# Attention and a greedy mixture of experts on one core: route 1's logits ahead of a branch, another form of the threshold rounds, another order of the first weight steps, and two GpSimd drains

## The chip, the core and the metric

The kernel runs on one core of a Trainium2 chip. Its engines are TensorE (PE, matrix products; its weight loads are listed as PEld), VectorE (DVE), ScalarE (ACT), GpSimd (POOL) and SyncE (SP), which issues most DMAs; each works through its own queue in order. The metric is the device time of one execution in microseconds, as the median of several runs.

## The reference

Eight batches of eight heads, 576 positions of 64 elements, go through attention with a mask in blocks of 64. The result, as 4608 tokens of 512, goes through a mixture of eight experts with a greedy assignment: all 4608 × 8 logits are walked through in falling order, and a token goes to an expert if it has none yet and the expert has fewer than 576 tokens.

```python
# attention: scores = q k^T / 8, masked where block(i) < block(j); softmax; times v
x = attn_out.transpose(0, 2, 1, 3).reshape(4608, 512)
logits = x @ w_gate
for idx in np.argsort(-logits.flatten()):
    tok, e = idx // 8, idx % 8
    if assigned[tok] >= 0 or counts[e] >= 576: continue
    assigned[tok] = e; counts[e] += 1
for e in range(8):
    mask = assigned == e
    out[mask] = np.maximum(x[mask] @ w1[e], 0.0) @ w2[e]   # 512 -> 1024 -> 512
```

## The kernel before, in words

**Attention** takes about the first 342 us. It leaves x in DRAM as two 16-bit halves (high and low) and the logits in SBUF as 128 partitions × 36 tokens × 8 experts. No line of it is changed.

**Eight routes** then give each expert its tokens, one expert a route. Every token proposes itself to the best expert that is still open. Route k finds for each open expert the 576th largest proposed logit, takes the expert whose threshold is highest, marks its tokens, and takes them and the expert out of the logits (`Lm`) for route k+1. The threshold is found in `rounds`: 14 rounds, each cuts an interval to a quarter. One round is: three thresholds (`cd`, L782 on DVE); how many logits lie above each, counted per partition by two DVE instructions (`jk`, L790, with the counts by accumulation) and one ACT instruction (`ja`, L759); the sums over partitions on PE (`tot`, L806); the choice of the step from them (`sg`, L809, DVE). `CB` (L792) is the lower end of the interval, which grows by the step chosen. In round 6 the search goes over to a shifted copy of the logits (`m_P`). Route 0 has another form: four quick rounds and a test whether they suffice, then a branch (`If`, L942) whose rarely taken side has the other rounds. Route 7 needs no rounds.

**From marks to rows**: `place` and `invert` turn the marks into a list of 576 token numbers by PE products (`pe` L977, `ps` L984) and DVE steps (`OH`, `OL`, `RH`, `ixt`, `ix`; RH is the last operand of `pe` on DVE). POOL gathers the rows in five indirect DMAs of 128 (the last of 64) rows (`xg`, L1050). For experts 0 and 1 PE transposes them (`xt`, L1062) and DVE (L1067) and ACT (L1066) copy them out as `X`; for the others SP's DMA transposes.

**Weights** of an expert come in 12 pieces of 512 KB from SP's DMAs (`raw`, L990) and are split into 16-bit halves. The first four pieces of experts 0 and 1 are split by one ACT step each (L1007) and one DVE step (L1009); all others by ACT (L1014, L1018) and POOL (L1020). For expert 0 the first four pieces are asked for as soon as its number is known, ahead of the branch.

**FFN** of an expert: `h` on PE (L1102, three passes over halves) in two groups of columns (128 and 448 for expert 0, else 256 and 320), its relu as halves `HH` by ACT (L1088) and `HL` by DVE (L1090), then `y` on PE (L1127, and L1131 for the 64 rows of tile m=4), out of PSUM by ACT (L1110) and for m=4 also DVE (L1114), and a scatter to the output on POOL, an indirect DMA per tile m (L1118). The last expert takes its tiles in the order 0, 1, 2, 4, 3.

**Order.** The kernel writes each engine's order itself: every piece of work is a generator whose `yield` names an engine, a cost in ns and events to wait for, and a greedy list scheduler `Sched` picks what is issued next by costs, events and priorities (a smaller number goes first). Costs, event times (`sc.ev`) and `sc.busy` change nothing but the order. Route k+1 and expert k+1's weights are worked on beside the FFN of expert k, so their instructions stand among each other in the queues; waiting is done by semaphores.

**Before the change at the branch**: route 0's index list is made (the `invert` ahead of L942), the result of the test is loaded (`values_load`, L970), and all engines concerned branch. Behind it come eight warming matmuls (L953), the weight steps of expert 0, the gathers and X copies; a generator `out` (made in `route`) waits until the fourth weight piece of expert 0 is split, then takes the chosen expert and its tokens out of `Lm` (L913 to L930) and starts route 1, which begins with the best open logit per token (`vm`, L728), proposals (`nP` L744, `PV` L746), and their transposed copy `PB`, by PE (`rt`, L750), ACT (L754) and DVE (L751).

## Time and profile before

| | |
|---|---|
| timed runs | 788.42, 785.0, 785.38 us; median 785.38 |
| profiled execution, its own time | 788.48 us |
| its span, first to last instruction | 786.6 us |
| mean granted PE clock in it | 0.969 |
| attention | about 0 to 342 us |
| first h of the experts 0, 1, 2, 3 | 365.27, 427.25, 480.95, 531.46 us |
| index product `pe` of routes 0 and 1 | 357.53, 411.78 us |
| last scatter issued; last instruction | 778.18; 786.6 us |

A row of the timeline reads: start, duration, engine, line, operation, output <- input, shapes, count, and in brackets the idle time ahead of it with what ended it. Neighbouring equal instructions are shown as one row. In a row of stretches stand start and end, length, then busy time with instruction count for PE, PEld, DVE, ACT and POOL, the granted PE clock, the share of DMA engines in use, and GB/s. Some rows show a name with "q" behind the engine: instructions of its sequencer, such as a wait, a drain or a branch. Line numbers in brackets of the form L1118 belong to the kernel before; the changed kernel's are up to 16 higher or one lower.

### The profile page before, as it was taken

How to read it: one execution, taken by the hardware profiler on the slowest of the kernel's cores; microseconds unless marked ns; L12 is line 12 of the kernel's file. 1: busy time of each engine (PE TensorE's matmuls, PEld its weight loads, DVE VectorE, ACT ScalarE, POOL GpSimd, SP SyncE). 2: the span in 40 equal slices, each digit the busy share in tenths (PEclk: the TensorE clock that was granted, in tenths of full speed). 3: DMA queues.
4: the chain of work that ended last, by engine and by line, in shares of the span. 5: the costliest groups of instructions: out<-in, count | busy, mean ns of one | idle time of the engine just before them, and what ended most of it. 6: DMA issues, size and time to landing. Idle time of an engine off the chain costs nothing.

```text
span 786.6 us, 19035 instructions
## 1 busy us (share of the span) xinstructions
PE 724.0 (92%) x6532; PEld 480.4 (61%) x6532; DVE 563.5 (72%) x2295; ACT 540.7 (69%) x1456; POOL 465.2 (59%) x515
## 2 busy tenths in 40 slices
PE   5789998899989999957997999999999999999995
PEld 3566776667766777735544756647557475574752
DVE  6899788998899879666988878969688692430210
ACT  5788878888988898735835859495965948391210
POOL 5788887898889877512414348184661927675001
PEclk9899999999999999977997999999999999999998
DMA  9879999989999994258026066391935719771001
GB/s 202 162 151 176 213 193 209 157 158 226 195 213 168 224 187 90 77 124 273 9 95 237 5 235 154 125 246 47 291 92 186 177 68 279 237 172 50 22 22 38
DMA packets 244354, 121.66 MB, mean 155 GB/s; under 512 B 200832, under 2 KB 227328, under 8 KB 244256
## 3 DMA queue, kind: packets, MB, share of 16 engines
q1 hardware_dynamic: 238320, 101.42, 57.0%
q0 software_dynamic: 5936, 19.01, 7.5%
q8 instruction: 52, 0.85, 0.5%
q14 instruction: 46, 0.38, 0.1%
HBM read 71.45 MB, written 18.87 MB: 115 GB/s over the span
## 4 chain that ended last, share of the span: by engine, by line
PE 40%; DMA 6%; POOL 3%; ACT 2%; issue 2%; DVE 1%; SPq 0%; POOLq 0%; ACTq 0%
PE h L1102 22%; PE y L1127 14%; DMA raw<-in_moe_w_dram 4%; PE y L1131 3%; POOL W L1020 1%; POOL xg L1050 1%; DMA xg<-x,ix 1%; ACT W L1018 1%; PE pe L977 1%; ACT ja L759 1%; ACT raw L1014 1%; PE tot L806 0%; DMA out_dram<-yo,ix 0%; SPq L990 0%; ACT HH L1088 0%
## 5 line engine op out<-in xcount | busy, mean ns | idle before, releaser
L438 POOL TENSOR_TENSOR P<-P,m 128x320 f32<-128x320 f32 (+8 forms) x285 | 208.6, 766 | 51.4 <-DVE m L430 34.6
L1102 PE MATMUL h<-X,W 128*128 128x320 f16 (+3 forms) x1536 | 198.5, 289 | 0.2 <-DVE HL L1090 0.2
L1102 PEld LDWEIGHTS <-W 128*128 128x128 f16 x1536 | 142.7, 98 | 42.8 <-issue 1.5
L416 ACT ACTIVATE P<-psb,m 128x576 f32<-128x576 f32 (+8 forms) x288 | 149.2, 542 | 26.3 <-DVE m L409 17.3
L1127 PE MATMUL y<-W,HH 128*128 128x512 f16 x512 | 152.4, 379 | 0.0
L1020 POOL TENSOR_TENSOR W<-raw,W 128x1024 f16<-128x1024 f32 x56 | 118.2, 2135 | 30.0 <-ACT W L1018 26.2
L405 DVE TENSOR_REDUCE m<-psb 128x1 f32<-128x576 f32 (+8 forms) x288 | 125.1, 481 | 14.5 <-PE psb L380 14.0
L463 PE MATMUL psb<-mident,P 128*128 128x128 f32 x800 | 107.0, 283 | 11.0 <-POOL P L438 3.8
L380 PEld LDWEIGHTS <-qT 128*64 128x64 f16 x1408 | 78.8, 114 | 44.1 <-issue 29.3
L1118 POOL DMA_INDIRECT out_dram<-yo,ix x40 | 38.8, 970 | 108.6 <-ACT yo L1110 71.9
L380 PE MATMUL psb<-kT,qT 128*64 128x288 f16 (+8 forms) x704 | 92.9, 289 | 9.8 <-ACT P L416 9.3
L463 PEld LDWEIGHTS psb<-mident,P 128*128 128x128 f32 x800 | 88.1, 143 | 22.6 <-POOL P L438 6.6
L498 PE MATMUL psb<-PT,V 128*64 128x448 f32 (+5 forms) x776 | 98.1, 391 | 2.2 <-DVE PT L446 1.7
L1088 ACT ACTIVATE HH<-h 128x320 f16<-128x320 f32 (+3 forms) x128 | 51.8, 408 | 67.1 <-PE h L1102 59.8
L1127 PE MATMUL y<-W,HL 128*128 128x512 f16 x256 | 97.1, 379 | 0.0
L1050 POOL DMA_INDIRECT xg<-x,ix x40 | 39.9, 999 | 90.6 <-DMA raw<-in_moe_w_dram 48.1
L444 ACT ACTIVATE PT<-psb 128x512 f32<-128x512 f32 (+1 forms) x165 | 82.7, 592 | 6.6 <-PE psb L463 6.2
L380 PE MATMUL psb<-kS,qT 128*64 128x288 f16 (+8 forms) x704 | 85.4, 287 | 1.7 <-DVE kS L350 1.5
L1090 DVE SCALAR_TENSOR_TENSOR HL<-h,HH 128x320 f16<-128x320 f32 (+3 forms) x128 | 57.5, 452 | 39.3 <-ACT HH L1088 39.1
L1127 PEld LDWEIGHTS <-HH 128*128 128x128 f16 x512 | 46.8, 97 | 52.6 <-issue 1.7
L1014 ACT ACTIVATE raw<-raw 128x512 f32<-128x512 f32 x112 | 67.4, 624 | 8.1 <-DMA raw<-in_moe_w_dram 8.1
L498 PEld LDWEIGHTS psb<-PT,V 128*64 128x64 f32 x776 | 49.8, 138 | 33.3 <-issue 24.3
(234 smaller groups left out, 1038.9 us busy)
## 6 DMA issues: line engine op xcount, KB each, us to landing
raw<-in_moe_w_dram SPq DMA_DIRECT2D x64, 512.0 KB, 5.5
x<-XR SPq DMA_DIRECT2D x8, 1152.0 KB, 5.5
kn<-in_k_dram SPq DMA_DIRECT2D x15, 576.0 KB, 4.9
qn<-in_q_dram SPq DMA_DIRECT2D x15, 576.0 KB, 7.2
V<-in_v_dram SPq DMA_DIRECT2D x64, 128.0 KB, 4.4
V<-in_v_dram SPq DMA_DIRECT2D x16, 64.0 KB, 3.7
xg<-x,ix POOLq DMA_INDIRECT x41, 4.4
out_dram<-yo,ix POOLq DMA_INDIRECT x40, 2.8
```

Source lines behind the costliest of these rows:

```text
L380: nc.tensor.matmul(out if len(K1.shape) == 2 else out.rearrange("p (r j) -> p r j", r=2), lhsT=A[:, h, 64 * i:64 * i + 64], rhs=K1, start= ...
L405: nc.vector.tensor_reduce(m[:, 0, c:c + 1], ps[:, o:o + 64 * (i + 1)] if g else s.part(ps, g, i, o), axis=AX.X if g else AX.XY, op=OP.max)
L416: nc.scalar.activation(out, in_, AF.Exp, bias=m[:, 1, c:c + 1], scale=s.ESC, accum_out=m[:, 2, c:c + 1])
L438: nc.gpsimd.tensor_tensor(sl, sl, m[:, 3, c:c + 1].to_broadcast([P, w]), op=OP.mult)
L444: s.nc.scalar.activation(out, in_, AF.Copy)
L463: nc.tensor.transpose(ps[:, a], s.Pb[n % s.NP][:, s.OFF[i] + 128 * j:s.OFF[i] + 128 * j + P], s.ident)
L498: nc.tensor.matmul(ps[64 * h:64 * h + 64, 64 * (i0 - b0):64 * (b1 - b0)], lhsT=vn[:, j, 2 * (n % 2) + h, :], rhs=pt[:, s.PTI[(j, i0)]:s.PT ...
L1014: nc.scalar.activation(raw[:,x],raw[:,x],AF.Copy,scale=s.WS)
L1020: nc.gpsimd.tensor_tensor(lw,raw,hi,op=OP.subtract)
L1090: nc.vector.scalar_tensor_tensor(HL[:,f,ts],ps,0.0,HH[:,f,ts],op0=OP.max,op1=OP.subtract)
L1102: nc.tensor.matmul(ps,lhsT=W[:,a,d,f*P:f*P+P],rhs=X[:,4*(d//2)+d%2+l,ts],start=(d==0 and n==0),stop=(d==3 and n==2))
L1127: if m<4: nc.tensor.matmul(ps,lhsT=Z[:,f,m*P:m*P+P],rhs=Y[:,a,f],start=(f==n==0),stop=(f==7 and n==2))
```

## The change

1. **Rounds** of routes 1 to 6: each threshold used to be lower end + step + multiple of the width, in three instructions after the step `sg` is known. Now the three sums without the step (`base`, `bs`) are made at the end of the round before, by three instructions from that round's thresholds (three memsets in round 6, where the search starts from zero again), and after `sg` one instruction adds the step to all three. It has an accumulator output that is not used. The lower end `CB` is no longer kept from round to round, but made from the first threshold in rounds 6 and 13.
2. **Route 1's logits**: `winner` makes them (in a tile of their own, `L_1`) and the best per token ahead of the branch, on DVE between RH and the copy of `pe`; the branch's other side makes them again after its own rounds. Behind the branch route 1 starts at once. Two waits given to the scheduler for route 1, and 1500 ns in PE's account, are gone.
3. **First weights' steps**: other times, costs and priorities in the scheduler, which put the ACT and DVE splits of expert 0's first four pieces elsewhere among the X copies.
4. **Drains**: after the m=4 scatter of the last two experts POOL executes a `drain`.

```diff
--- before.py
+++ after.py
@@ route @@
-        yield D,369 if k else 30,('Lm',k),('mid',k-2),('wc',0,s.GW) if k==1 and s.GW>=0 else None
-        if k: V.tensor_reduce(vm,Lm,axis=AX.X,op=OP.max)
+        yield D,369 if k>1 else 30,('Lm',k),('mid',k-2)
+        if k>1: V.tensor_reduce(vm,Lm,axis=AX.X,op=OP.max)
...
-                yield T,214,'rt',('xm',0,s.GS) if k==1 and s.GS>=0 else None
+                yield T,214,'rt'
@@ rounds @@
-                        yield D,70 if k==0 else 210,('P2',k) if PBx is not PB else None
+                        yield D,70 if k==0 else 140,('P2',k) if PBx is not PB else None
                         if k==0: V.tensor_tensor(cand[:,2:3],base[:,2:3],nw,op=OP.add)
-                        else:
-                            for i in (2,0,1): V.tensor_scalar(cand[:,i:i+1],lo,nw,(i+1)*w,op0=OP.add,op1=OP.add)
+                        else: V.tensor_scalar(cand,base,nw,0.0,op0=OP.add,op1=OP.add,accum_out=s.ab)
...
-                    if t: add(lo,lo,nw)
+                    if k:
+                        if t==s.NSC: V.tensor_scalar(CB[:,0:1],cand[:,0:1],-w,None,op0=OP.add)
+                        if t==s.NS-1: V.tensor_scalar(CB[:,1:2],cand[:,0:1],-w,None,op0=OP.add)
+                    elif t: add(lo,lo,nw)
...
                     if t==s.NS-1: add(CB[:,2:3],CB[:,0:1],lo)
-                    elif k==0:
+                    else:
                         base=rp.tile([P,3],F32,tag="base",name=f"bs{k}_{t}")
-                        V.tensor_scalar(base,s.io3,wk[:,t+1:t+2],lo,op0=OP.mult,op1=OP.add)
-                    if live: sc.busy(D,330 if k==0 else 150)
+                        if k==0: V.tensor_scalar(base,s.io3,wk[:,t+1:t+2],lo,op0=OP.mult,op1=OP.add)
+                        elif t==s.NSC:
+                            for i in range(3): V.memset(base[:,i:i+1],(i+1)*w/4)
+                        else:
+                            for i in (2,0,1): V.tensor_scalar(base[:,i:i+1],cand[:,i:i+1],-(i+1)*3*w/4,None,op0=OP.add)
+                    if live: sc.busy(D,330)
@@ route, behind the rounds @@
+        def winner():
+            V.tensor_tensor(es,s.es,ei,op=OP.subtract)
+            V.tensor_scalar(u,oh,-8.0,None,op0=OP.mult)
+            V.tensor_scalar(q[:,3],MM[:,0],8.0,None,op0=OP.mult)
+            V.tensor_tensor(L1,Lm,be(u),op=OP.add)
+            V.tensor_tensor(L1,L1,b3(q[:,3]),op=OP.subtract)
+            V.tensor_reduce(vm,L1,axis=AX.X,op=OP.max)
...
             def out():
-                yield D,600,('wc',0,3) if k==0 else None
-                mk=MM[:,0]
-                if k==0: full()
-                else:
-                    V.tensor_tensor(q[:,2],q[:,2],MM[:,0],op=OP.add); mk=q[:,2]
-                V.tensor_scalar(q[:,3],mk,8.0,None,op0=OP.mult)
+                yield D,600
+                V.tensor_tensor(q[:,2],q[:,2],MM[:,0],op=OP.add)
+                V.tensor_scalar(q[:,3],q[:,2],8.0,None,op0=OP.mult)
...
-            s.ask(eidx); more.__exit__(None,None,None)
+            winner(); s.ask(eidx); more.__exit__(None,None,None)
...
-            for n in range(4): sc.ev['wl',0,n]=max(sc.ev['ask',0]+4500+1150*n,sc.now)
+            for n,t in enumerate((5200,6500,8200,10400)): sc.ev['wl',0,n]=sc.ev['ask',0]+t
...
-            sc.free[T]=max(sc.free[T],sc.now)+213*s.NWU+1500
-            sc.add(s.late(),0,sc.now)
+            sc.free[T]=max(sc.free[T],sc.now)+213*s.NWU
+            s.Lm,s.es=L1,es; sc.set(('Lm',1))
+            sc.add(s.route(1),0,sc.now)
@@ invert: at its end the line goes on with @@
+        if live and k==0: s.rv=nc.values_load(...); s.winner(); sc.busy(D,1900)
@@ weights @@
-                sc.add(conv(n,raw,hi,lw,('wc',k,n)),2,sc.now)
+                sc.add(conv(n,raw,hi,lw,('wc',k,n)),-1 if k==0 and n<4 else 2,sc.now)
@@ flip @@
-            for j in range(2): sc.add(ev(j),0,sc.now)
+            for j in range(2): sc.add(ev(j),k-2,sc.now)
@@ ffn, behind the scatter @@
+            if m==4 and k>s.E-3: nc.gpsimd.drain()
```

What the scheduler makes of it, in three places. First, DVE from the last operand of route 0's `pe` to the branch; before:

```order
L967 TENSOR_TENSOR RH_5389<-OH_5388,m_tok 128x720
L970 TENSOR_LOAD m_5270
L980 CAST ixt_5438<-pe_5401 128x40
L986 CAST ix_5370<-ps_5440 128x5
L942 COMPARE_AND_BRANCH
```

and with the change (L920 to L925 are `winner`; L995 and L1001 the copies of `pe` and `ps`):

```order
L982 TENSOR_TENSOR RH_5391<-OH_5390,m_tok 128x720
L985 TENSOR_LOAD m_5270
L920 TENSOR_TENSOR es_5372<-m_es,m_5270 128x1
L921 TENSOR_SCALAR u_5272<-f_5269 128x8
L922 TENSOR_SCALAR q_5367<-MM_5265 128x36
L923 TENSOR_TENSOR L_5371<-m_Lm,u_5272 128x288
L924 TENSOR_TENSOR L_5371<-L_5371,q_5367 128x288
L925 TENSOR_REDUCE m_vm<-L_5371 128x36
L995 CAST ixt_5446<-pe_5409 128x40
L1001 CAST ix_5370<-ps_5448 128x5
L956 COMPARE_AND_BRANCH
```

Six instructions stand ahead of the first copy that were behind the branch.

Second, DVE behind the branch; before (W_0 are the weight steps, X the copies, L913 to L930 route 1's logits):

```order
L1009 SCALAR_TENSOR_TENSOR W_0_5735<-raw_0_5355,W_0_5735 128x1024
L1009 SCALAR_TENSOR_TENSOR W_0_5735<-raw_1_5356,W_0_5735 128x1024
L1067 COPY X_5737<-xt_0_5749 128x4x128
L1009 SCALAR_TENSOR_TENSOR W_0_5735<-raw_2_5357,W_0_5735 128x1024
L1067 COPY X_5737<-xt_1_5762 128x4x128
L1009 SCALAR_TENSOR_TENSOR W_0_5735<-raw_3_5358,W_0_5735 128x1024
L1067 COPY X_5737<-xt_2_5786 128x4x128
L913 TENSOR_TENSOR m_es<-m_es,m_5270 128x1
L914 TENSOR_SCALAR u_5272<-f_5269 128x8
L915 TENSOR_TENSOR m_Lm<-m_Lm,u_5272 128x288
L929 TENSOR_SCALAR q_5367<-MM_5265 128x36
L930 TENSOR_TENSOR m_Lm<-m_Lm,q_5367 128x288
```

and with the change:

```order
L744 TENSOR_TENSOR m_nP<-L_5371,m_vm 128x288
L746 SCALAR_TENSOR_TENSOR PV_5758<-m_nP,L_5371 128x288
L751 STREAM_TRANSPOSE m_PB<-PV_5758 128x32
...
L1024 SCALAR_TENSOR_TENSOR W_0_5749<-raw_0_5355,W_0_5749 128x1024
L1024 SCALAR_TENSOR_TENSOR W_0_5749<-raw_1_5356,W_0_5749 128x1024
L1082 COPY X_5751<-xt_0_5781 128x4x128
L1024 SCALAR_TENSOR_TENSOR W_0_5749<-raw_2_5357,W_0_5749 128x1024
L1082 COPY X_5751<-xt_1_5801 128x4x128
L789 TENSOR_SCALAR jk_0_0_5839,cn_0_5797<-m_PB,bs_5769 128x288
L1024 SCALAR_TENSOR_TENSOR W_0_5749<-raw_3_5358,W_0_5749 128x1024
```

Route 1's proposals and their transposed copy now stand ahead of the weight steps, and the first counts of its round 0 among them.

Third, one round of route 1 on DVE among the first FFN; before (CB is the lower end of the interval, m_P the shifted logits):

```order
L792 TENSOR_SCALAR CB_5910<-CB_5910,sg_9_6279 128x1
L809 SCALAR_TENSOR_TENSOR sg_10_6304<-tot_10_6299,m_wk 128x3
L782 TENSOR_SCALAR cd_11_6307<-CB_5910,sg_10_6304 128x1 x3
L790 TENSOR_SCALAR jk_11_0_6315,cn_11_6306<-m_P_5237,cd_11_6307 128x288
L790 TENSOR_SCALAR jk_11_1_6318,cn_11_6306<-m_P_5237,cd_11_6307 128x288
L792 TENSOR_SCALAR CB_5910<-CB_5910,sg_10_6304 128x1
```

and with the change (bs is the base for the next round):

```order
L1105 SCALAR_TENSOR_TENSOR HL_5813<-h_6_1_6248,HH_5812 128x448
L815 SCALAR_TENSOR_TENSOR sg_10_6300<-tot_10_6295,m_wk 128x3
L781 TENSOR_SCALAR cd_11_6303,m_ab<-bs_10_6286,sg_10_6300 128x3
L789 TENSOR_SCALAR jk_11_0_6309,cn_11_6302<-m_P_5237,cd_11_6303 128x288
L789 TENSOR_SCALAR jk_11_1_6316,cn_11_6302<-m_P_5237,cd_11_6303 128x288
L808 TENSOR_SCALAR bs_11_6318<-cd_11_6303 128x1 x3
L1105 SCALAR_TENSOR_TENSOR HL_5813<-h_7_1_6280,HH_5812 128x448
L815 SCALAR_TENSOR_TENSOR sg_11_6332<-tot_11_6327,m_wk 128x3
```

Three instructions between step and first count have become one; behind the counts stand three where one stood.

More of the change, by code (lines that the diff above doesn't have):

```diff
@@ L933, in route @@
             s.late=out
+            if k==0:
+                L1=rp.tile([P,C,E],F32,name="L_1",bufs=1); es=rp.tile([P,1],F32,name="es_1",bufs=1)
+                s.winner=winner
         yield from place(1 if last or k==0 else 2)
@@ L969, in invert @@
         if live and 0<k<s.E-1: sc.add(s.late(),0,sc.now)
-        if live and k==0: s.rv=nc.values_load(s.m1[0:1,1:2].bitcast(I32),engines=s.IFE,skip_runtime_bounds_check_because="0 or the bits of 1.0")
+        if live and k==0: s.rv=nc.values_load(s.m1[0:1,1:2].bitcast(I32),engines=s.IFE,skip_runtime_bounds_check_because="0 or the bits of 1.0"); s.winner(); sc.busy(D,1900)
         s.hold(k)
@@ L1005, in conv @@
             if k<2 and n<4:
-                yield A,947,('wl',k,n)
+                yield A,1060 if k==0 else 947,('wl',k,n)
                 nc.scalar.activation(hi,raw,AF.Copy,scale=s.WS)
-                yield D,1135,('ix',k),('xm',0,0) if k==0 and n in s.XC else None
+                yield D,1140,('ix',k),('xm',0,0) if k==0 and n in s.XC else None
                 nc.vector.scalar_tensor_tensor(lw,raw,s.WS,hi,op0=OP.mult,op1=OP.subtract)
@@ L1038, in weights @@
                 if k or n>3: sc.dma(1456,('wl',k,n))
-                sc.add(conv(n,raw,hi,lw,('wc',k,n)),2,sc.now)
+                sc.add(conv(n,raw,hi,lw,('wc',k,n)),-1 if k==0 and n<4 else 2,sc.now)
                 n+=1
-    WS=32.0; XS=64.0; NWU=8; NWA=5; NWM=0; GW=-1; GS=2; XC=()
+    WS=32.0; XS=64.0; NWU=8; NWA=5; NWM=0; XC=()
     def gather(s,k,ix):
@@ L1052, in gather @@
             if k==1: sc.ev['xg',k,m]+=2500
-            if k==0: sc.ev['xg',k,m]=sc.now+1900
+            if k==0: sc.ev['xg',k,m]=sc.now+2400
             sc.nolat()
@@ L1063, in ev @@
             def ev(j):
-                yield (A,480) if j else (D,600)
+                yield (A,520) if j else (D,380 if k==0 else 600)
                 o,i=X[:,4*j:4*j+4,m*P:m*P+n],ps[:,4*j:4*j+4,:n]
```

## The prediction

> **What bounds the kernel now.** I began with the page: its shares, then the chain that ended last.
>
> ```profile
> span 786.6 us, 19035 instructions
> PE 724.0 (92%) x6532; PEld 480.4 (61%) x6532; DVE 563.5 (72%) x2295; ACT 540.7 (69%) x1456; POOL 465.2 (59%) x515
> ```
>
> The mean says TensorE (PE), but a change in the routing has to be judged from its own stage, so the busy time by stretches came next (length, PE busy, then the other engines, and the granted clock before the DMA share):
>
> ```profile
> 419.00:431.00 12.00, 6.85 (x56) 4.84 (x57) 9.68 (x45) 5.50 (x14) 4.00 (x5) 0.71 0.54 193
> 431.00:481.00 50.00, 50.00 (x371) 30.54 (x369) 38.57 (x207) 38.62 (x94) 25.23 (x17) 0.97 0.47 136
> 481.00:531.00 50.00, 49.81 (x380) 30.45 (x382) 41.55 (x227) 37.76 (x92) 28.72 (x20) 1.00 0.63 166
> 531.00:582.00 51.00, 50.59 (x386) 30.69 (x382) 38.32 (x205) 36.70 (x88) 32.91 (x22) 1.00 0.53 158
> ...
> 730.00:772.00 42.00, 42.00 (x291) 27.12 (x290) 8.02 (x17) 8.95 (x20) 3.79 (x4) 1.00 0.07 24
> ```
>
> From 431 on PE is full: expert after expert, it waits for next to nothing (0.2 to 0.4 us in each of the stretches shown). Time can be won there only by less PE work (there is none here), by starting it earlier, or after it. The one hole is 419 to 431, between the first expert's FFN and the second's. The timeline of PE shows its shape:
>
> ```profile
> 411.78 0.92 PE L977 MATMUL pe<-RH,OL 128*32 128x40 f16 x36
> 421.68 0.62 PE L1062 MATMUL xt<-m_idh,xg 128*128 128x128 f16 x8 [1.54 <-DMA xg<-x,ix]
> 424.00 1.03 PE L1062 MATMUL xt<-m_idh,xg 128*128 128x128 f16 x8 [1.35 <-DMA xg<-x,ix]
> 427.25 2.10 PE L1102 MATMUL h<-X,W 128*128 128x256 f16 x9
> 430.42 0.80 PE L1102 MATMUL h<-X,W 128*128 128x256 f16 x3
> ```
>
> PE waits for gathered rows, which wait for route 1's index list (`pe`). Then nine h matmuls run and PE stands until 430.42, because the fourth weight step of expert 1 is late on VectorE (DVE), behind the rounds of route 2. And the hole costs clock too:
>
> ```profile
> 427.86 1.22 DVE L1009 SCALAR_TENSOR_TENSOR W<-raw,W 128x1024 f16<-128x1024 f32 x1
> 422.00:424.00 2.00, 0.48 (x7) 0.23 (x5) 1.97 (x11) 0.65 (x2) 0.60 (x1) 1.00 1.01 337
> 426.00:428.00 2.00, 2.00 (x21) 1.63 (x19) 0.69 (x5) 1.14 (x4) 0.52 (x1) 0.50 0.01 2
> 434.00:436.00 2.00, 2.00 (x19) 1.76 (x18) 1.58 (x9) 1.26 (x4) 0.00 (x0) 0.93 0.00 0
> ```
>
> PE is granted half speed from about 424 to 434.3. So h's progress at full speed began effectively at 430.42 + 1.9 (3.85 us at half) − 1.0 (the nine early matmuls, 2.10 at half) = **431.3**.
>
> The end of the program is a second place:
>
> ```profile
> 773.62 0.90 POOL L1118 DMA_INDIRECT out_dram<-yo,ix  x1 [2.52 <-DVE yo L1114]
> 778.18 0.96 POOL L1118 DMA_INDIRECT out_dram<-yo,ix  x1 [3.67 <-ACT yo L1110]
> 773.62 2.60 DMA out_dram<-yo,ix
> L1191 POOLq DRAIN  x3: 45/108/7883, 778.0 to 786.4; - x3
> ```
>
> (The third row is from the chain: issue to landing.) GpSimd's (POOL's) last scatter should land at 778.18 + 2.6 to 2.7 = 780.9, yet the longest of its three drains takes 7.88 us, to 785.9, and the span ends at 786.6. So 5 us pass in which no data moves.
>
> **The change part by part.**
>
> *Route 1's logits ahead of the branch.* Before, they were made among the first expert's copies:
>
> ```profile
> 358.53 0.20 DVE L980 CAST ixt<-pe 128x40 f16<-128x40 f32 x1 [2.09 <-PE pe L977]
> 368.25 0.46 DVE L915 TENSOR_TENSOR m_Lm<-m_Lm,u 128x288 f32<-128x288 f32 x1
> 369.54 0.44 DVE L728 TENSOR_REDUCE m_vm<-m_Lm 128x36 f32<-128x288 f32 x1
> 373.27 0.51 DVE L790 TENSOR_SCALAR_CACHE_REDUCE jk<-m_PB,bs 128x288 f16<-128x288 f32 x1 [1.29 <-ACT m_PB L754]
> 375.07 0.15 DVE L809 SCALAR_TENSOR_TENSOR sg<-tot,m_wk 128x3 f32<-128x3 f32 x1
> 402.96 0.16 DVE L809 SCALAR_TENSOR_TENSOR sg<-tot,m_wk 128x3 f32<-128x3 f32 x1
> ```
>
> The six instructions (some 1.7 us, three of them 0.45) now run in the 2.09 us in which DVE waits for `pe`: price nothing. Without that cover they would delay the first gather, and with it everything, by 1.7. What follows (nP, PV, PB: 1.1 us) comes right after the branch. DVE then has, from 359.5 to the first step choice `sg`: these 1.1, four weight steps at 1.22 (the row at 427.86), four X copies at 0.42, two counts at 0.44, and small memsets and bases, in all about 9.7: **sg at 369.2 instead of 375.07, −5.9**. That needs no weight step to wait for its data. The first FFN's own h loses nothing by it: its start is bound by gathers and the same four steps. I take its second half as starting where it did.
>
> Thirteen rounds lie between first and last `sg`. If each becomes 0.11 to 0.22 longer on a full DVE (below), 1.4 to 2.9 of the 5.9 go: `pe` moves by −4.5 to −3.0. PE's order gives the same upper end: `pe` now stands in y tile 2 and not 3, some 20 matmuls earlier, which at the pace of the chain's longest y pieces are 4.5 us:
>
> ```profile
> 473.46 2.61 PE y L1127 x12
> ```
>
> I take **−3.7**.
>
> The last landing moves with it, and the fourth weight step of expert 1 ends at 429.08 − 3.7 = 425.4. The gaps of PE that remain (waits for five gathers, with transposes between) are shorter, so I count no half clock: h starts effectively at 425.3 instead of 431.3, **−6.0**. If the half clock stays it is −4.0.
>
> By the Trainium skill's page "TensorE: Matmul & The Clock Gate" (Part 1) a free-running window of 3413 ns that is idle drops PE to half speed; the 10.2 us at 0.5 here are three such windows, which agrees. By it the gain depends on whether a remaining gap fills a window.
>
> *One instruction for three thresholds.* One round of before, where DVE was not full, and the nearest rows for the new form (a pointer scalar, with accumulation, and what depends on it):
>
> ```profile
> 395.42 0.46 DVE L782 TENSOR_SCALAR cd<-CB,sg 128x1 f32<-128x1 f32 x3
> 395.80 0.51 DVE L790 TENSOR_SCALAR_CACHE_REDUCE jk<-m_P,cd 128x288 f16<-128x288 f32 x1
> 396.67 0.21 DVE L792 TENSOR_SCALAR CB<-CB,sg 128x1 f32<-128x1 f32 x1
> 397.06 0.16 DVE L809 SCALAR_TENSOR_TENSOR sg<-tot,m_wk 128x3 f32<-128x3 f32 x1 [0.19 <-PE tot L806]
> 353.56 0.20 DVE L884 TENSOR_SCALAR_CACHE_REDUCE f<-tx,m 128x8 f32<-128x8 f32 x1
> 353.69 0.08 DVE L884 DVE_READ_ACCUMULATOR f<-tx,m 128x1 f32 x1
> 353.81 0.23 DVE L885 TENSOR_SCALAR f<-f,m 128x8 f32<-128x8 f32 x1
> ```
>
> From the three thresholds to the first count: 0.38 before, 0.25 by the nearest rows: −0.13 on the path of a round that waits only for itself. But the bases of the next round are three instructions (3 × 0.12 = 0.37 of issue) where one (0.12) stood: +0.25 on DVE. In a round that waits for nothing but DVE the balance is 0.37 + 0.25 − 0.38 − 0.12 = about +0.11; if the accumulator's read isn't overlapped, +0.22. Which of the two holds depends on how full DVE is:
>
> ```profile
> 375.00:403.00 28.00, 28.00 (x155) 13.77 (x154) 25.87 (x143) 19.01 (x49) 9.50 (x5) 1.00 0.03 10
> 437.00:452.00 15.00, 15.00 (x127) 11.56 (x126) 14.49 (x80) 14.60 (x39) 6.43 (x4) 1.00 0.01 2
> ```
>
> Full stretches like the second take about 25 of the 65 rounds of routes 2 to 6 (I found 52 us of them), so some 2.8 us more on DVE there; but PE is full beside it and has work of its own queued. What shows of it is that route 2 starts earlier relative to PE's work by less than PE does: FFN 1 gives back 1 to 2 us in `tot` waits. I take **+1.5**. Later experts stop PE little today. Expert 2 has the least to spare: POOL's last three weight steps end at 480.2, and its h starts at 480.95.
>
> ```profile
> 473.90 6.31 POOL L1020 TENSOR_TENSOR W<-raw,W 128x1024 f16<-128x1024 f32 x3
> 480.95 2.13 PE L1102 MATMUL h<-X,W 128*128 128x256 f16 x18
> ```
>
> With h due 4 us earlier, these steps, which follow the gathers, must come earlier too; I count +0.4 for that and what comes later.
>
> The Trainium skill ("VectorE: DVE Perf Modes", Rules for kernel authors) says to minimize the count of operations on DVE. Here the count of a round goes from four small ones to four plus a read, so the rule speaks against this edit; by it the rounds lose, as the rows for a full DVE do too.
>
> *Order of the first weights' steps.* It moves ACT's and DVE's shares of expert 0's conversion among the X copies. Its durations stay, DVE has the order that the sum above used, and its cover is the PE hole after each gather. I cost it at nothing; bounds ±1, since the first h groups wait for an X copy or a weight step 0.2 to 0.9 us each today.
>
> *The drains.* Two are added on POOL, behind the m=4 scatters of the last two experts.
>
> ```profile
> 732.98 0.91 POOL L1118 DMA_INDIRECT out_dram<-yo,ix  x1 [3.71 <-DVE HL L1090]
> 759.83 0.96 POOL L1118 DMA_INDIRECT out_dram<-yo,ix  x1 [25.94 <-ACT yo L1110]
> ```
>
> The first stands behind 733.9, and POOL then has nothing to do for 25.9 us: any price up to that is hidden. The second begins at 774.5, and the last scatter comes 3.7 us later. No trace shows a drain after one or few indirect DMAs. Bounds for the last one: below, 0.1 (the median of the drains above); above, the 6.7 that the long one needs after its last instruction (785.9 − 779.1). If the price is for what has piled up since the start (81 indirect DMAs, some 83 ns each), the first drain pays it under cover, the second is short, and the last waits for the landing alone: 780.9 + 0.5 + 0.8 (barrier) = 782.2, **−4.4**. I take this end, since 5 us without any data moving look like bookkeeping that grows with use. The Trainium skill ("VectorE: DVE Perf Modes", The DRAIN you can't avoid) gives the boilerplate drains as some 12 ns and constant. The long one here measures 7.88 us, so it isn't of that kind; by the page nothing would be won at the end.
>
> *Sum* against the profiled 788.48: −6.0 + 1.5 + 0.4 − 4.4 = −8.5, so 780.0. Of the three timed runs two lie 3.1 to 3.5 below that execution, the third beside it. Part of such a difference may be half-clock time that I have counted already, so I take 2.0 off: **778.0 us**.
>
> **The rivals.**
> A: *the last drain stays as long as it was*, because its price belongs to the end of the program. For it: the barrier of all engines stands there too. Against it: the 7.88 us belong to POOL alone. 778.0 + 4.4 = 782.4.
> B: *every drain after a scatter has a fixed price of some 6.7.* The second would last from 774.5 to 781.2, the last scatter would go 3.0 later than at 778.18, and the last drain is as long as before: +3.1 in the tail, so 778.0 + 4.4 + 3.1 = 785.5. For it: only one such drain was ever seen, so nothing tells price from backlog.
> C, the slower one: *DVE becomes the bound of all rounds.* PE's queue is in order: each `tot` stands among FFN matmuls, and a round longer than the work between two of them stops PE. Price: 0.22 in each of the 65 rounds is 14.3, so 778.0 + 14.3 = 792.3. It decides slower from 0.17 a round (11.3 us in all). Against it: beyond the full stretches DVE idles about 1 us a round, and the first half of a round is shorter.
> D: *the earlier start buys nothing*, since the hole is only moved: route 2's rounds reach PE's queue as late as ever. 778.0 + 4.1 = 782.1 with the tail's gain.
>
> **How the numbers follow.** Forecast 0.53, A 0.20, B 0.12, C 0.08, D 0.07. Below 0.5% (some 4 us, about what a measurement of this kernel can tell) nothing counts as a change: faster means under 781.45, slower over 789.3. The forecast's own range is 775 to 781: `pe` −4.5 to −3.0 with ±1 for the first weights, half clock or not (2.0), and 1 to 3.5 for profiled against timed. It is nearly all faster; a third of A and D are too (0.09): faster 0.62. C is slower, the rest the same: 0.08 and 0.30. The range 773.5 to 785.0 takes in the forecast with 2 us below its own range for a price of rounds of nothing (+1.5 and +0.4 gone), A, D and half of B; C and the other half of B stay out.
>
> **What would show it.** Route 1's first `sg` near 369 and its last near 399.6; `pe` of route 1 near 408; PE's hole from the first FFN's last y to h without `tot` waits, and no half clock there, with h from 425 at the latest; the threshold instruction to first count at 0.25; full stretches longer by 0.1 a round. At the end: a drain of several us under the idle of POOL behind 733 (its time moved by the front), a short one near 770, and the last one under 3 us. The prediction is wrong if the long drain is still last, if `tot` waits in the second FFN exceed 4 us, or if the weight steps of expert 2, whose last ends within 1 us of its h today, stop PE.

## The result, and the profile after

The changed kernel takes 779.33 us (median of 9 runs, 776.85 to 783.51) against 786.35 us of the kernel before (9 runs): a ratio of 0.990 with a 95% interval of 0.987 to 0.993. In a later comparison, on other runs of both, it was 776.82 against 787.35 us, 0.986 (0.983 to 0.989). The forecast was 778.0 us in a range of 773.5 to 785.0, and faster: the measured time lies 1.3 us above it, inside the range.

The profiled execution takes 776.85 us. First its span and the stretches (length, then busy time of PE, PEld, DVE, ACT and POOL, the granted clock, DMA share):

```profile
span 775.1 us, 19128 instructions
...
413.00:427.00 14.00, 11.62 (x100) 6.75 (x99) 9.57 (x50) 7.00 (x18) 3.27 (x4) 0.88 0.56 199
427.00:477.00 50.00, 50.00 (x387) 31.27 (x385) 40.80 (x251) 39.77 (x99) 25.62 (x17) 1.00 0.51 147
477.00:527.00 50.00, 49.37 (x377) 30.42 (x376) 38.31 (x227) 37.94 (x94) 30.67 (x20) 1.00 0.59 160
...
726.00:768.00 42.00, 42.00 (x277) 25.70 (x276) 7.59 (x16) 8.27 (x19) 4.57 (x5) 1.00 0.07 23
```

The hole is still there, smaller: PE is idle for 2.4 us of it and not 5.2, at a mean clock of 0.88 and not 0.71. PE's timeline shows what it waits for:

```profile
406.22 0.93 PE L992 MATMUL pe<-RH,OL 128*32 128x40 f16 x36
417.62 0.62 PE L1077 MATMUL xt<-m_idh,xg 128*128 128x128 f16 x8 [0.59 <-DMA xg<-x,ix]
419.85 0.77 PE L1077 MATMUL xt<-m_idh,xg 128*128 128x128 f16 x8 [1.61 <-DMA xg<-x,ix]
424.51 0.50 PE L1117 MATMUL h<-X,W 128*128 128x256 f16 x3
```

Still the gathers; the wait ahead of h is gone. Some of the first expert's y matmuls stand behind the transposes now and fill the gap.

Cores start the routing at slightly different times in each execution (the attention is untouched), so I count from the index product `pe` of route 0: 357.53 before, 355.24 after, a difference of 2.3 that has nothing to do with the change (in the other traces kept here it comes at 353.1 to 359.0, with either front). What lies between that `pe` and the last scatter I call the front, what lies behind the last scatter the tail.

| from route 0's `pe` (us) | before | after | after, second execution |
|---|---|---|---|
| first `sg` of route 1 | 17.5 | 12.3 | 12.7 |
| `pe` of route 1 | 54.2 | 51.0 | 50.4 |
| effective start of h, expert 1 | 73.8 | 69.3 | 67.1 |
| h of expert 2 | 123.4 | 118.9 | 116.8 |
| last scatter issued | 420.7 | 415.8 | 413.1 |
| from there to the span's end | 8.4 | 4.0 | 4.0 |

So of the 11.5 us between the two profiled spans 2.3 lie ahead of the change, 4.8 in the front and 4.4 in the tail. The front differs from execution to execution: the three traces of the old front (the kernel before and two experiments on it) have the last scatter at 419.3, 420.7 and 422.1, so that the front's gain is known to some 1.5 us. The tail, in POOL's instructions and drains (L1135 are the added two, L1207 the final ones):

```profile
725.89 0.90 POOL L1133 DMA_INDIRECT out_dram<-yo,ix  x1 [3.75 <-DVE HL L1105]
752.70 0.96 POOL L1133 DMA_INDIRECT out_dram<-yo,ix  x1 [25.90 <-ACT yo L1125]
...
766.80 0.90 POOL L1133 DMA_INDIRECT out_dram<-yo,ix  x1 [2.50 <-DVE yo L1129]
771.05 0.96 POOL L1133 DMA_INDIRECT out_dram<-yo,ix  x1 [3.35 <-ACT yo L1125]
L1135 POOLq DRAIN  x2: 3042/5225/7408, 725.7 to 766.6; - x2
L1207 POOLq DRAIN  x3: 51/108/3021, 770.8 to 774.8; - x3
```

The drain at 725.7 lasts 7.4 us, inside the 25.9 that POOL has nothing to do; the one at 766.6 lasts 3.0 and ends ahead of the last scatter; the final one lasts 3.0 instead of 7.9.

### The profile page after: what moved, and what is told of

It reads as the page before. It is cut to its first block, busy times and chain, and to the rows that moved or that the text cites. A ratio compares the mean times of both kernels' runs of the same rounds, so it can differ in the third digit from the quotient of the medians.

```text
span 775.1 us, 19128 instructions
## 1 busy us (share of the span) xinstructions
PE 715.9 (92%) x6532; PEld 477.3 (62%) x6532; DVE 557.2 (72%) x2385; ACT 540.1 (70%) x1456; POOL 464.5 (60%) x515
## 4 chain that ended last, share of the span: by engine, by line
PE 44%; DMA 4%; POOL 2%; issue 2%; ACT 2%; POOLq 0%; SPq 0%; ACTq 0%
PE h L1117 24%; PE y L1143 16%; PE y L1147 2%; DMA raw<-in_moe_w_dram 2%; POOL xg L1065 1%; DMA xg<-x,ix 1%; POOL W L1035 1%; PE pe L992 1%; ACT W L1033 1%; ACT ja L759 0%; DMA out_dram<-yo,ix 0%; ACT raw L1029 0%; POOL out_dram L1133 0%; ACT yo L1125 0%; PE tot L812 0%
## 5 line engine op out<-in xcount | busy, mean ns | idle before, releaser
L1117 PE MATMUL h<-X,W 128*128 128x320 f16 (+3 forms) x1536 | 194.6, 286 | 0.8 <-DVE X L1082 0.5
L405 DVE TENSOR_REDUCE m<-psb 128x1 f32<-128x576 f32 (+8 forms) x288 | 125.0, 481 | 11.6 <-PE psb L380 11.1
L380 PEld LDWEIGHTS <-qT 128*64 128x64 f16 x1408 | 76.9, 111 | 43.0 <-issue 28.3
L380 PE MATMUL psb<-kT,qT 128*64 128x288 f16 (+8 forms) x704 | 90.3, 283 | 10.9 <-ACT P L416 9.8
L380 PE MATMUL psb<-kS,qT 128*64 128x288 f16 (+8 forms) x704 | 82.7, 280 | 1.7 <-DVE kS L350 1.5
```

What stands on the lines that cost most here:

```text
L380: nc.tensor.matmul(out if len(K1.shape) == 2 else out.rearrange("p (r j) -> p r j", r=2), lhsT=A[:, h, 64 * i:64 * i + 64], rhs=K1, start= ...
L405: nc.vector.tensor_reduce(m[:, 0, c:c + 1], ps[:, o:o + 64 * (i + 1)] if g else s.part(ps, g, i, o), axis=AX.X if g else AX.XY, op=OP.max)
L1117: nc.tensor.matmul(ps,lhsT=W[:,a,d,f*P:f*P+P],rhs=X[:,4*(d//2)+d%2+l,ts],start=(d==0 and n==0),stop=(d==3 and n==2))
```

## The experiments

My theory ahead of the runs: the tail's gain is the drains', by a price per indirect DMA that is paid early; the front's gain is route 1's earlier start; the rounds' new form and the order of the first weights are worth nothing. The runs undo or isolate one part each.

**The drains.** First, the changed kernel without them:

```diff
-            if m==4 and k>s.E-3: nc.gpsimd.drain()
```

> The changed kernel without its two drains, else the same instructions in the same order. Theory (the final drain's long price is paid early by the first added drain, under POOL's idle time): the tail from the last scatter's issue to the end goes from 4.05 back to 8.4 us, the last drain lasts 7.4 to 7.9 us, the time is about 783.7 (+4.4). Rival (the tail became shorter for another reason than the drains, such as the chip or the execution): last drain near 3 us, time within 1 us of 779.3.

Measured: 781.91 us, ratio to the kernel before 0.9946 (0.9924 to 0.9969); the profiled span's tail is 8.5 us. Then the kernel before with the two drains alone:

```diff
+            if m==4 and k>s.E-3: nc.gpsimd.drain()
```

> The kernel before with the two drains alone. Theory (the two gains add up): the drain behind the seventh expert's m=4 scatter lasts about 7.4 us in idle time, the one behind the last expert's m=4 and the final one 3 us each; time 786.35 - 4.4 = 782.0. Rival (the early drain only pays off together with the moved work): time within 1 us of 786.35.

Measured: 783.4 us, 0.9949 (0.9928 to 0.997), tail 4.0 us. Their longest drains, without (L1206, final) and with (L1120, the added two; L1192, final):

```profile
L1206 POOLq DRAIN  x3: 45/108/7885, 775.3 to 783.7; - x3
```

```profile
L1120 POOLq DRAIN  x2: 3034/5221/7408, 729.0 to 769.2; - x2
L1192 POOLq DRAIN  x3: 51/108/3032, 773.8 to 777.8; - x3
```

The tail comes and goes with the drains, with either front: half of the gain of the changed kernel, 0.5%. What the price goes by, one early drain in the kernel before tells:

```diff
+            if m==1 and k==0: nc.gpsimd.drain()
```

> The kernel before with one drain, behind the second scatter of the first expert (about 405 us), where POOL then stands idle for 8.7 us, after 8 of the 81 indirect DMAs. Theory (the price grows with the indirect DMAs since the last drain, 4.9 us behind the landing for 81, so 0.06 each): the early drain ends about 0.5 us behind its landing (3.2 us long), the final one is still 7.3 us. Rival (only the first drain after an indirect DMA is dear, once): the early one takes 7 to 8 us, the final one 3 us, and the time is 4.4 below the kernel before.

Measured, a single run (788.04 us beside 789.15 of the kernel before):

```profile
404.30 0.97 POOL L1118 DMA_INDIRECT out_dram<-yo,ix  x1 [4.25 <-ACT yo L1110]
413.97 1.00 POOL L1050 DMA_INDIRECT xg<-x,ix  x1 [8.70 <-DVE ix L986]
L1120 POOLq DRAIN  x1: 4372/4372/4372, 404.1 to 404.1; - x1
L1192 POOLq DRAIN  x3: 51/108/7221, 778.1 to 785.9; - x3
```

A first drain does not make later ones cheap. With 73 indirect DMAs behind the early one, the final drain ends at 785.36, 4.3 us behind the last landing (estimated from its issue at 778.37 and 2.7 us); with 81, in the kernel before, it was 785.83 − 780.89 = 4.9. That is 0.059 and 0.061 us each; the changed kernel's first added drain, with 76, ends 4.6 behind its landing (733.08 − 728.51), 0.060 each. The short ones there, with 4 and 1, end 0.1 to 0.2 behind theirs. So a drain waits for the landing and then takes 0.06 us per indirect DMA since the last drain; the rival of a one-time price falls, and with it that of a fixed one. The early drain itself lasted 4.4 us, to 408.43. Its landing is not marked in the trace, but its DMA packets are: the last one in the software queue, which carries the indirect DMAs, ends at 407.59. In the marked cases the landing comes 0.35 behind that (728.17 and 728.51 for the drain with 76), so that 0.5 us are left for 8 DMAs, 0.06 each again. What the runs don't part is a price per DMA from one per row, since each of them moves 128 rows (every fifth 64).

**The front, without the earlier logits.** The changed kernel with route 1's logits behind the branch, the order of the first weights kept:

```diff
-                yield D,600
+                yield D,600,('wc',0,3) if k==0 else None
...
-            winner(); s.ask(eidx); more.__exit__(None,None,None)
+            s.ask(eidx); more.__exit__(None,None,None)
...
-            s.Lm,s.es=L1,es; sc.set(('Lm',1))
-            sc.add(s.route(1),0,sc.now)
+            sc.add(s.late(),0,sc.now)
```

> The changed kernel with route 1's logits made behind the branch, after the fourth weight step, as before; rounds, drains and first order as changed. Theory (the earlier logits carry all of the front's gain): first step choice of route 1 17.5 us and its index product 54 to 55 us behind the index product of route 0 (now 12.3 and 51.0), first h of expert 1 at 73 to 74 (now 69.3), time 779.3 + 4.5 = 783.8. Rival (the order of the first weights carries half of the gain): time 781.5 or less. Rival (the hole is bound by the gathers' transfers anyway): within 1 us of 779.3.

Measured: 783.02 us, 0.9945 (0.9926 to 0.9965), what the drains alone give. The timelines of PE and DVE:

```profile
356.86 0.94 PE L983 MATMUL pe<-RH,OL 128*32 128x40 f16 x36 [1.54 <-DMA raw<-in_moe_w_dram]
412.44 0.92 PE L983 MATMUL pe<-RH,OL 128*32 128x40 f16 x36
426.74 1.49 PE L1108 MATMUL h<-X,W 128*128 128x256 f16 x6
```

```profile
375.14 0.15 DVE L815 SCALAR_TENSOR_TENSOR sg<-tot,m_wk 128x3 f32<-128x3 f32 x1
```

From route 0's `pe` that is 18.3 to the first `sg`, 55.6 to route 1's `pe`, and the last scatter comes at 421.6: the whole front is lost; 421.6 lies among the 419.3 to 422.1 of the old front. One expectation failed: h of expert 1 starts at 69.9 and not at 73 to 74. But it starts at half clock (0.50 granted from 426 to 428), and h of expert 2 comes at 123.2, where the kernel before has 123.4.

**The front, without the order.** The changed kernel with the old times, costs and priorities of the first weights:

```diff
-            for n,t in enumerate((5200,6500,8200,10400)): sc.ev['wl',0,n]=sc.ev['ask',0]+t
+            for n in range(4): sc.ev['wl',0,n]=max(sc.ev['ask',0]+4500+1150*n,sc.now)
...
-                sc.add(conv(n,raw,hi,lw,('wc',k,n)),-1 if k==0 and n<4 else 2,sc.now)
+                sc.add(conv(n,raw,hi,lw,('wc',k,n)),2,sc.now)
```

> The changed kernel with the old times, costs and priorities of the first weights' steps in the scheduler: DVE then does the first two rounds of route 1 ahead of the second to fourth weight step, and PE's order has the index product of route 1 some 7 us of FFN work earlier than the changed kernel (29.4 instead of 36.5). Theory (the new order is what lets the early route 1 pay: without it the weight steps are late and the first FFN waits in its first half): second half of the first FFN 4 us later than with the change or more, time 781 or more. Rival (the order of the first weights is worth nothing): 779.3 within 0.7. Second rival (the earlier index product closes the hole further): 777.5 or less.

Measured: 783.04 us, 0.9914 (0.9893 to 0.9936); this chip's kernel before took 789.15, so the ratio by itself doesn't tell it from the changed kernel's first 0.990. On the same chip the changed kernel with some repeated transposes (below) took 778.75, 0.9866 (0.9848 to 0.9884), which is clearly less. The trace shows why; PE first, then DVE:

```profile
356.95 0.95 PE L992 MATMUL pe<-RH,OL 128*32 128x40 f16 x36 [1.54 <-DVE L L923]
371.86 0.18 PE L812 MATMUL tot<-cn,m_bo 128*128 128x3 f16 x1 [1.92 <-DVE jk L789]
373.18 2.53 PE L1117 MATMUL h<-X,W 128*128 128x128 f16 x22 [0.97 <-DVE W L1024]
380.03 0.73 PE L1117 MATMUL h<-X,W 128*128 128x448 f16 x3
```

```profile
371.90 1.21 DVE L1024 SCALAR_TENSOR_TENSOR W<-raw,W 128x1024 f16<-128x1024 f32 x1
```

DVE runs route 1's first rounds ahead of the third and fourth weight step, the third starts only at 371.90, and h waits for it. The second half of the first FFN (448 columns) starts 23.1 us behind `pe` and not 18.2; route 1's index product is earlier still (48.8), which helps nobody; the last scatter comes at 420.5, among those of the old front. So the two halves of the front need each other: by these traces, one execution each, neither the earlier logits nor the order is worth anything alone, and together they are 4.8 to 7.6 us. The times agree for the logits; for the order they leave room for a rest, since the drains alone gave 0.9949 (0.9928 to 0.997).

**The rounds' form.** The changed kernel with the old rounds:

```diff
-                        else: V.tensor_scalar(cand,base,nw,0.0,op0=OP.add,op1=OP.add,accum_out=s.ab)
+                        else:
+                            for i in (2,0,1): V.tensor_scalar(cand[:,i:i+1],lo,nw,(i+1)*w,op0=OP.add,op1=OP.add)
...
-                        else:
-                            for i in (2,0,1): V.tensor_scalar(base[:,i:i+1],cand[:,i:i+1],-(i+1)*3*w/4,None,op0=OP.add)
```

> The changed kernel with the old form of the rounds (three instructions for the thresholds, no bases) and its old costs in the scheduler; PE's order in route 1 is the same. Theory (the pace of the rounds is set by where tot stands in PE's queue, and the DVE work differs by less than 0.1 us a round): rounds of 1.97 us in the y stage as before, index product of route 1 at the same distance (51.0 us) from that of route 0 within 0.3, time 779.3 within 0.5. Rival (the new form's shorter path carries part of the gain, 0.12 in each of 13 rounds): that distance 52.5, time 780.9 or more. Second rival (the new form costs DVE 0.1 a round): time 778 or less.

Measured: 778.79 us, 0.9903 (0.9875 to 0.9931); route 1's `pe` at 50.4, the last scatter at 416.6. Nothing is lost without the new form. A round of the changed kernel in the y stage shows why:

```profile
394.81 0.27 DVE L808 TENSOR_SCALAR bs<-cd 128x1 f32<-128x1 f32 x3
395.44 0.16 DVE L815 SCALAR_TENSOR_TENSOR sg<-tot,m_wk 128x3 f32<-128x3 f32 x1 [0.36 <-PE tot L812]
395.52 0.08 DVE L815 DVE_READ_ACCUMULATOR sg<-tot,m_wk 128x1 f32 x1
395.64 0.22 DVE L781 TENSOR_SCALAR_CACHE_REDUCE cd<-bs,sg 128x3 f32<-128x3 f32 x1
395.78 0.08 DVE L781 DVE_READ_ACCUMULATOR cd<-bs,sg 128x1 f32 x1
395.90 0.51 DVE L789 TENSOR_SCALAR_CACHE_REDUCE jk<-m_P,cd 128x288 f16<-128x288 f32 x1
```

Thresholds to count are 0.26 us, 0.12 shorter; but DVE waits 0.36 for `tot` and not 0.19, and `sg` to `sg` is 1.97 (393.47 to 395.44), as in the last three rounds of the kernel before: `tot` stands at a fixed place among the y matmuls, and the round takes as long as PE takes to get there. The opposite edit writes the three bases twice:

```diff
                             for i in (2,0,1): V.tensor_scalar(base[:,i:i+1],cand[:,i:i+1],-(i+1)*3*w/4,None,op0=OP.add)
+                            for i in (2,0,1): V.tensor_scalar(base[:,i:i+1],cand[:,i:i+1],-(i+1)*3*w/4,None,op0=OP.add)
```

> The changed kernel with the three base instructions of each round written twice (same values), in an unchanged order: DVE has 0.19 us more in each of 65 rounds of routes 2 to 6 and in 12 of route 1. Theory (where tot stands in PE's queue sets the pace, DVE has 0.4 us and more of slack in most rounds): time 779.3 within 1.0. Rival (my slower case: DVE sets the pace of all rounds): 0.19 x 65 = 12 us, 791. Between (only the 25 or so rounds in which DVE is full): up to +4.8.

Measured: 781.44 us, 0.990 (0.9859 to 0.994), too wide to tell. In the traces, from the first h of expert 1 to that of expert 7, it takes 302.1 us where the changed kernel takes 298.4 and 297.8 (old form: 298.4). The list of those who waited for the bases' line names the reason: the weight load of `tot` (PEld) waited 5.8 us in 13 cases for the first three bases (and 2.1 in 5 for the second three), in the changed kernel 2.1 us in 5 for its only three.

```profile
  PEld L813: 5.8, 13
```

```profile
  PEld L812: 2.1, 5
```

So DVE is near the edge: in this one execution 0.19 us more a round cost 4 us, which is about what 25 full rounds would (4.8), not 65 (12).

**What is left of the hole.** Two edits on the changed kernel. One keeps PE busy in it by repeating the transposes of expert 1's tiles 1 and 2:

```diff
+            for _ in range((1,2,3,1,1)[m] if k==1 else 1):
             for j in range(8): nc.tensor.transpose(ps[:,j,:n],xg[:n,P*j:P*j+P],s.idh[:n,:n])
```

> The changed kernel with the PE transposes of the second expert's gathered tiles 1 and 2 written two and three times (same values), so that PE works 1.8 us more in the hole between the first two FFNs. Theory (the half clock behind the hole comes from PE's idle time in it): granted clock 1.0 from 410 on, first h of expert 1 at 67.6 to 68.3 behind the index product of route 0 (now 69.3) and time 778 to 778.6. Rival (the hole is bound by the gathers' landing, and half clock hits only waiting): no gain in the time, 779.3 within 0.5, clock 1.0 or not. Second rival (the added work delays the copies of X): 780 or more.

Measured: 778.75 us, 0.9866 (0.9848 to 0.9884). The clock in the hole is full:

```profile
413.00:427.00 14.00, 12.56 (x129) 8.01 (x127) 10.59 (x53) 8.13 (x19) 4.09 (x5) 1.00 0.64 232
```

But h starts at 68.7, and the last scatter comes at 417.4. The changed kernel in its second execution had full clock without any filling and h at 67.1:

```profile
413.00:427.00 14.00, 11.77 (x113) 7.42 (x112) 11.05 (x56) 8.28 (x20) 4.33 (x5) 1.00 0.59 213
```

With gaps of this size the half clock comes in some executions and not in others, and I can't say that filling pays. The other edit asks for the fifth and later weight pieces of expert 1 behind its gathers:

```diff
+                elif k==1 and n==4:
+                    yield S,25,'hw',('wc',0,6),('fl',1)
+                    yield G,60,('gi',1)
+                    raw=wp.tile([P,1024],F32,tag="raw",name=f"raw{k}_{wd}_{d}",bufs=6)
+                    nc.gpsimd.memset(raw[:,0:1],0.0)
+                    yield S,25,'hw'
```

> The changed kernel with the fifth and later weight pieces of expert 1 asked for only behind its gathers (a small POOL write into the buffer makes SP's DMA wait for POOL). In the changed kernel pieces five and six land at 413.1 and 416.0, the gathers 6.3 to 7.4 us after their issue. Theory (the hole that is left is bound by the gathers, which share the DMA engines with these pieces): gathers land within 5 us of their issue, first h of expert 1 at 67 to 68 behind the index product of route 0, time 1 to 2 below the changed kernel on the same chip. Rival (the gathers are bound by their own queue): landing unchanged, time within 0.5. Second rival (the late pieces stop expert 1's y): slower by 1 or more.

> The changed kernel once more, as the measure for the other three on the same chip. Theory: 6 to 10 below the kernel before, as measured; its first h of expert 1 at 68 to 70 and its last scatter at 415.5 to 417 behind the index product of route 0.

Measured on one chip: 775.32 us, 0.9847 (0.9817 to 0.9876), against 776.82, 0.9858 (0.9831 to 0.9886), for the changed kernel again. The gathers' times from issue to landing (minimum, median, maximum of five), first of the edit, then of the change again:

```profile
DMA to landing us min/median/max: 3.1/3.6/3.9
```

```profile
DMA to landing us min/median/max: 5.9/6.4/7.2
```

The transfers do collide, and without it the gathers take little more than half. Yet h moves only from 67.1 to 66.2, since the first expert's last y matmuls and X copies stand ahead of it, and 1.5 us in the time lie within the intervals. It is the fastest kernel that was run, but not shown to be faster than the change.

**A cheaper base, which was not.** Since more DVE work cost time, less should win some: the three bases as one instruction.

```diff
-                            for i in (2,0,1): V.tensor_scalar(base[:,i:i+1],cand[:,i:i+1],-(i+1)*3*w/4,None,op0=OP.add)
+                            V.scalar_tensor_tensor(base,s.io3,-3*w/4,cand,op0=OP.mult,op1=OP.add)
```

> The changed kernel with the three base instructions of a round as one (constant times width plus thresholds), in an unchanged order. Theory (a few of the rounds wait for DVE, as twice the base cost some 2 us): DVE has about 0.1 us less a round, the time is 0.5 to 1.2 below that of the changed kernel on the same chip. Rival (nothing depends on it any more): within 0.4.

Measured: 813.62 us, **slower**, 1.0345 times the kernel before (1.0302 to 1.0389) and 37 us above the changed kernel on the same chip. With the filled hole it was the same:

> The changed kernel with both edits: base in one instruction, and the repeated transposes that keep PE busy in the hole. Theory (the hole's half clock costs up to 1.7 us, and later rounds give back less of it when DVE has less to do): 1 to 2 below the changed kernel on the same chip. Rival (what is won ahead of the second FFN is lost to the tot waits behind it): within 0.7.

Measured: 815.29 us, 1.0349 (1.0317 to 1.0382). The instruction as a group, and one of them beside POOL's timeline:

```profile
L808 DVE SCALAR_TENSOR_TENSOR bs<-m_io,cd 128x3 f32<-128x3 f32 x66 | 56.0, 849 | 0.0
...
467.53 1.78 DVE L808 SCALAR_TENSOR_TENSOR bs<-m_io,cd 128x3 f32<-128x3 f32 x1
470.64 6.16 DVE L808 SCALAR_TENSOR_TENSOR bs<-m_io,cd 128x3 f32<-128x3 f32 x1
478.13 0.16 DVE L808 SCALAR_TENSOR_TENSOR bs<-m_io,cd 128x3 f32<-128x3 f32 x1
```

```profile
467.14 2.14 POOL L1035 TENSOR_TENSOR W<-raw,W 128x1024 f16<-128x1024 f32 x1
470.49 6.28 POOL L1035 TENSOR_TENSOR W<-raw,W 128x1024 f16<-128x1024 f32 x3
```

Three elements per partition take 0.16 us alone, and 6.16 us when POOL is splitting weights: 23 of 72 were held, each until 0.02 to 0.03 us behind the end of a POOL step (467.53 + 1.78 = 469.31 against 469.28), 55.7 us in all; none of the other 49 lay beside such a step for more than 0.06 us. Rounds then wait, and PE behind them: its `tot` waits 23.8 us from 420 to 670, and h of expert 5 comes 308.5 us behind route 0's `pe` where the changed kernel has 270.4.

## Why the prediction was right, and where it was not

- **Tail, −4.4.** Measured 8.4 to 4.0, by the mechanism that I took: 7.4 us hidden under POOL's 25.9, the second and the last drain 3.0 each. The end that I chose between 0.1 and 6.7 (a price by what has piled up, 83 ns each) was right in kind; measured are 60 ns each behind the landing. Rivals A and B fell with the changed kernel's own profile (its second and its last drain take 3.0 us), and the runs with and without the drains confirm it. The Trainium skill ("VectorE: DVE Perf Modes", The DRAIN you can't avoid) gives boilerplate drains as some 12 ns and constant; measured are 7.9 and 3.0 us at the same place, so here the measurement decides.
- **The logits' cover.** The copy of `pe` now waits 0.28 us where it waited 2.09, so the six instructions cost nothing:

```profile
356.23 0.20 DVE L995 CAST ixt<-pe 128x40 f16<-128x40 f32 x1 [0.28 <-PE pe L992]
```

- **First `sg` −5.9, `pe` −3.7.** Measured −5.3 and −3.3 (in the second execution −4.8 and −3.8). What the rounds lose between the two has the size that I took, but not the reason: from the first to the last `sg` it is 27.9 us before and 29.9 and 28.9 after, yet 29.2 with the old form of the rounds too. So it isn't the new form's work that costs it; where `tot` stands in PE's queue in the first FFN is the likely cause, which no run isolates.
- **h −6.0.** Measured −4.5, in the second execution −6.7. Two of its steps failed. I took the first FFN's second half as starting where it did: it starts 18.2 us behind route 0's `pe` and not 17.0 (17.6 in the second execution), because `tot` of the early rounds stops PE in the first half, for 0.4, 0.4 and 0.9 us against 0.55 once before. The longest such wait, and the start of the second half (a row of several instructions shows the shape of the first alone; this one begins where the shape changes):

```profile
372.38 0.16 PE L812 MATMUL tot<-cn,m_bo 128*128 128x3 f16 x1 [0.93 <-ACT ja L759]
373.41 1.30 PE L1117 MATMUL h<-X,W 128*128 128x448 f16 x6
```

  And half clock did not vanish in the first execution (3.41 us of it, from 420.2), but did in the second. The better fit of y matmuls into the gap, which I had not seen in the order, probably made up for part of it; no run prices it.
- **Given back, +1.5 and +0.4.** Measured nothing: from h of expert 1 to h of expert 2 both take 49.6 (before: 431.3 to 480.95), and from there to the last scatter 297.2 before, 296.9 after. This step was wrong because the base was mis-sized: I priced each of its instructions at 0.12, by the thresholds' old rows; three of them take 0.19 in all (0.27 with their ends), so a full round has no more work than before. From the first h of expert 1 to that of expert 7 DVE is busy for 191.0 and 191.4 us, with the old form for 196.3: the full stretches did not become longer by 0.1 a round, as I had said. The two errors of the front, 1.5 us of gain too many and 1.9 of loss too many, nearly cancel, by luck.
- **Order of the first weights, nothing ±1.** Wrong as a price: undoing it takes all of the front away in the trace. It was right in the sum only because the 9.7 us of DVE work that I had added up were those of the new order.
- **Rival C.** Its mechanism is real, with the place and the size of the full stretches: 4 us for 0.19 more a round, in one execution. It did not decide, because the new form adds about nothing.
- **Rival D.** Fell with the table: h and everything behind it moved by 4.5.
- **Profiled against timed, −2.0.** The profiled execution before lay 2.1 above the median of the 9 runs, the one after 2.5 below its own. So the profiled executions differ by 11.6 us, 2.3 of them ahead of the change, and the medians by 7.0. The term was a guess about single executions; without it the forecast would have been 780.0, 0.7 high, with it it came out 1.3 low.

## What to carry to other kernels

A final drain whose length no transfer explains can be paid early: put a drain where its engine is idle, close to the end. Work that starts earlier must be costed together with the order of what it now competes with; here, by the traces, each half alone gained nothing. And where a small result goes through another engine's in-order queue, look first at its place there: here it set the pace, and shortening the path beside it gained nothing.

## What the runs showed of the hardware that I had not expected

A VectorE instruction that reads two tensors from SBUF was held as long as GpSimd's tensor operation ran, 2.1 us for one and up to 6.6 for several in a row, even with three elements. It isn't the operation: `sg`, the same one with its first tensor in PSUM, took at most 0.16 us in that run. The forms with one tensor input (thresholds, bases, counts) were not held either; in the changed kernel the shortest, median and longest of 198 bases, in ns:

```profile
L808 DVE TENSOR_SCALAR bs<-cd x198: 141/145/151, 368.9 to 632.1; 128x1 f32<-128x1 f32 x198
```

The Trainium skill ("SBUF — State Buffer", Who interferes with whom) says that a DVE instruction with two SBUF inputs contends with a GpSimd instruction that reads SBUF, over a pair of ports that is an exclusive lock; the trace agrees. What the trace adds is that GpSimd's next step, which starts some 0.07 us ahead of the end of the one before (three of 2.14 take 6.28), doesn't let the waiting instruction in between: 6.16 us for three steps.

A single tensor input is no safeguard, though. In the kernel before, a DVE instruction with one, of 36 elements, took 4.48 us instead of 0.18, to 0.04 us behind the second of two POOL steps; what sets it apart from the bases no run here tells.

```profile
674.15 4.48 DVE L909 TENSOR_SCALAR h<-q 128x36 f16<-128x36 f32 x1
674.38 4.21 POOL L1020 TENSOR_TENSOR W<-raw,W 128x1024 f16<-128x1024 f32 x2
```

And a GpSimd drain behind indirect DMAs costs 0.06 us for each of them since the last drain, after the last has landed, with no data moving: 0.5 us for 8, 4.3 for 73, 4.6 for 76, 4.9 for 81.
